# Where a 32x32 transpose takes its stride, and which PSUM bank a fold gives up

## The chip, the core and the metric

One core of a Trainium2 chip runs the whole program. The metric is device time in microseconds, the median of several runs. TensorE (PE) does the matmuls, ScalarE (ACT) and VectorE (DVE) do what lies between them, GpSimd (POOL) does a few subtractions and copies, SyncE (SP) issues most DMAs. PSUM, into which matmuls write, has eight banks of 128 x 512 fp32.

## What is computed

Three stages follow one another; the output of each is the input of the next.

```python
# attention with random features: 2 batches, 8 heads, 576 rows, 64 wide; 128 features
phi(x) = exp(h - max(h)) / sqrt(m),  h = x @ omega.T - sum(x*x)/2
num = phi(q) @ (phi(k).T @ v);  den = phi(q) @ sum(phi(k))
x = num / (den + 1e-6)                       # 1152 x 512
# gated product; w1, w2: 512 x 1024, w3: 1024 x 1024, w_out: 1024 x 512, in 64-bit floats
x = ((x @ w1) * (x @ w2)) @ w3 @ w_out
# four experts, weighted by normalised probabilities p
out = sum over e of p[:, e] * (relu(x @ ew1[e]) @ ew2[e])
```

## The kernel before

Products are computed in three passes over high and low halves of fp32 numbers: `split` (lines 79 to 82) makes a high half with a ScalarE copy and a low half with a VectorE subtraction (in some calls a GpSimd one), both from the same source.

**The attention** works on pairs of heads, eight of them (n = 0 to 7, four per batch). A pair transposes its keys and queries in bank `t`, computes features in the two banks `f`, sums keys with values in `kv`, transposes the exponentials of each of its two heads (`transpose_e`, line 449) in bank `et`, attends (`w` and `po` for the first two pairs, `x` and `kv` from the third), and places the result, transposed in bank `x`, in xt by a split. `attend_tail` does the same for the 64 left-over rows of a batch. A transpose in `et` fills a whole bank with one head, which ScalarE then copies to SBUF.

**The fold** (line 201) multiplies w3 with w_out ahead of time, so that the third stage's input takes one product fewer. There are eight folds, each over 128 rows of w3, in two halves of 12 matmuls into one bank, alternately `po` and `w`; then a split takes the result out of the bank. Each half needs one w3 tile, prepared by `fold_transposed` (line 184): four DMAs of 64-bit numbers, a ScalarE Prelu over the high words (line 100), a VectorE shift of the low words (line 101), a VectorE shift-and-or of the two (line 102), a VectorE transpose of 32x32 blocks (line 194), and a split (lines 81 and 82). Words of a 64-bit number alternate in SBUF, so a reader of the high words steps by 8 bytes. For w3 the columns are also regrouped, every fourth one together (`by_group`), which makes the step of the Prelu and the shift 32 bytes; what they write is contiguous, and so the transpose reads contiguously. The other weights (w1, w2, w_out) go through the same three lines without regrouping, at 8 bytes. Two tiles can stand ready for the fold (`bufs=2`).

**The order** comes from a scheduler that plays the program through with a cost model and takes instructions by priority, each engine's in one fixed order at the end. `BESIDE` (line 41) says which loads (o: w_out, w: w1 and w2), folds (f) and gated products (b) are traced beside which pair: fold 0 beside pair 2, folds 1 to 7 beside pairs 3 to 6, the gated products of batch 0 from pair 7 on, those in banks `w` and `po`. What stands beside a pair may not be issued on VectorE and ScalarE before that pair's query features. After the attention the remaining gated products (in all eight banks), the product with the folded weights, and the experts follow.

Of the kernel before, what the change touches and what calls it, by code (L numbers as in the profile page):

```python
# [8 lines left out]
F32 = mybir.dt.float32  # L9
# [3 lines left out]
ACTF = mybir.ActivationFunctionType  # L13
ALU = mybir.AluOpType
# [31 lines left out]
def attention_moe_kernel(ctx: ExitStack, tc: tile.TileContext, q, k, v, omega, mw1, mw2, mw3, mwo, probs, ew1, ew2, out):  # L46
    nc = tc.nc
# [5 lines left out]
    P = 128  # L53
# [22 lines left out]
    def bank(tag):  # L76
        return ps_p.tile([P, 512], F32, tag=tag, name="ps_" + tag, bufs=BANKS[tag])

    def split(hi, lo, src, eng=None):

        nc.scalar.activation(out=hi, in_=src, func=ACTF.Copy)  # L81
        (eng or nc.vector).tensor_tensor(out=lo, in0=src, in1=hi.bitcast(F32), op=ALU.subtract)  # L82

    def order_like(t, src):
        return t if len(src.shape) == 2 else t.rearrange("p (j g c) -> p j g c", j=src.shape[1], g=src.shape[2])

    def from_f64(srcs, name, order=lambda x: x):


        r = cv.tile([P, 512, 2], U32, tag="f64", name="f64", bufs=3)  # L90
        rows = P // len(srcs)
        for i, src in enumerate(srcs):
            o = r[i * rows:(i + 1) * rows].rearrange("p (k c) w -> p k (c w)", k=src.shape[1])
            nc.sync.dma_start(out=o, in_=src.bitcast(U32))
        low, high = order(r[:, :, 0]), order(r[:, :, 1])
        f = cv.tile([P, 512], F32, tag="f64f", name=name, bufs=2)
        e = cv.tile([P, 512], U32, tag="f64e", name="f64e", bufs=2)
        fb = f.bitcast(U32)

        nc.scalar.activation(out=order_like(f, high), in_=high.bitcast(F32), func=ACTF.Prelu, scale=2.0**-112, alpha=2.0**32)  # L100
        nc.vector.tensor_scalar(out=order_like(e, low), in0=low, scalar1=29, scalar2=None, op0=ALU.logical_shift_right)  # L101
        nc.vector.scalar_tensor_tensor(out=fb, in0=fb, scalar=3, in1=e, op0=ALU.logical_shift_left, op1=ALU.bitwise_or)
        return f

    def load_w64(pool, srcs, name, eng):
        f = from_f64(srcs, name + "f")
        t = pool.tile([P, 2, 512], F32R, tag=pool.name, name=name)
        split(t[:, HI], t[:, LO], f, eng=eng)
        return t
# [5 lines left out]
    def transpose(out, in_, rows=slice(0, P)):  # L115
        return nc.tensor.transpose(out, in_, ident[rows, rows])
# [67 lines left out]
    def fold_transposed(u):  # L184

        m, hf = divmod(u, KF // 4)
        rows = mw3[m * P:(m + 1) * P].rearrange("(j r) f -> r j f", r=SQ)
        first = [hf * 512 + i * P for i in range(4)]  # L190
        by_group = lambda x: x.rearrange("p (j c g) -> p j g c", j=4, g=4)
        r = from_f64([rows[:, :, f:f + P] for f in first], "w3f", by_group)
        t = cv.tile([P, 512], U32, tag="f64e", name="w3t", bufs=2).bitcast(F32)
        nc.vector.transpose(t, r)
        t = t.rearrange("p (j g r) -> p g j r", j=4, g=4)
        wt = cv.tile([P, 2, 512], F32R, tag="w3T", name="w3T", bufs=2)
        hi, lo = (wt[:, x].rearrange("p (g j r) -> p g j r", j=4, g=4) for x in (HI, LO))
        split(hi, lo, t)
        w3T.append(wt)

    def fold(m):

        po = bank(("po", "w")[m % 2])
        n = 0
        for hf in range(KF // 4):
            u = m * (KF // 4) + hf
            while len(w3T) < min(u + 2, KF * (KF // 4)):
                fold_transposed(len(w3T))
            for g in range(4):
                for a, c in PASSES:  # L210
                    nc.tensor.matmul(  # L211
                        out=po, lhsT=w3T[u][:, a, g * P:(g + 1) * P], rhs=wo[hf * 4 + g][:, c],
                        start=(n == 0), stop=(n == 3 * KF - 1),
                    )
                    n += 1
        t = w3_p.tile([P, 2, 512], F32R, tag="w3o", name="w3o", bufs=KF)
        split(t[:, HI], t[:, LO], po)
        w3o.append(t)
# [51 lines left out]
    with ExitStack() as actx:  # L270
# [75 lines left out]
        ps = bank("po")  # L346
# [6 lines left out]
        ps = bank("x")  # L353
# [10 lines left out]
        for b in range(B):  # L364
            t = st.tile([P, H, D1], F32, name=f"vt{b}")
# [18 lines left out]
        class Pair:  # L384
# [62 lines left out]
                nc.scalar.activation(out=self.kva, in_=ps[:, :2 * D1].rearrange("p (j d) -> p j d", j=2), func=ACTF.Copy)  # L447

            def transpose_e(self, j):
                ps = bank("et")  # L450
                self.eT[j] = at.tile([P, MAIN], F32, tag="eT", name="eT", bufs=2)
                for r in range(R):
                    transpose(ps[:, r * P:(r + 1) * P], self.of(self.eq, j, r))
                nc.scalar.activation(out=self.eT[j], in_=ps, func=ACTF.Copy)
# [75 lines left out]
        for n in range(len(pairs) + 1):  # L530
# [32 lines left out]
            with ExitStack() as order:  # L563

                for ins in (*u.mark, loaded) if u else ():
                    order.enter_context(tc.issue_after(ins))
                for s in BESIDE.get(n, "").split():
                    if s[0] == "w":
                        load_w12(int(s[1]))
                    elif s[0] == "o":  # L570
                        load_wo()
                    elif s[0] == "f":
                        fold(int(s[1]))
                    else:
                        gated(at, 2, int(s[1]), int(s[2]), ("w", "po") * 2)
# [319 lines left out]
```

## Time and profile before

| | us |
|---|---|
| median of 3 runs (lowest, highest) | 669.84 (669.25, 671.47) |
| the profiled execution's own time | 670.11 |
| its span, from the first to the last instruction | 668.3 |
| TensorE busy | 655.3 |
| VectorE busy | 463.4 |
| ScalarE busy | 422.0 |
| GpSimd busy | 122.8 |

All instants below count from the first instruction of the profiled execution. A row of the timeline gives start, duration, engine, line, operation, what it writes and reads, its form and how many were merged; in brackets, how long the engine stood idle before it and what released it. PEclk is the clock granted to TensorE as a share of 2.4 GHz; it has two levels, 1.00 and 0.50, and a value between them means that both occurred in the stretch. The merged groups by line give a number of instructions, their busy time and the mean of one, then the idle time before them. Matmuls are pipelined, and the ends of their rows are modelled.

### The profile page before, as it was taken

Reading aid. Unit: us, or ns where it says so; the run is one execution under the profiler, and the core shown is the slowest. Engines: PE = TensorE matmul, PEld = TensorE weight load, DVE = VectorE, ACT = ScalarE, POOL = GpSimd, SP = SyncE. Lnnn points to the kernel's source line nnn. Section 1 sums busy time; section 2 is a strip of 40 time slices with the busy share of each in tenths; the row PEclk is TensorE's granted clock in tenths of the full one; section 3 lists DMA queues with packets and bytes.
Section 4 is the critical chain, followed back from the end, with each engine's and each line's share of the span. In section 5 each row is a group of like instructions: output and inputs, shape, how many; then the busy total and the mean of one; then the engine's idle time right before and its main releaser. Section 6 shows DMA issues by size and latency. Waiting matters only on the chain.

```text
span 668.3 us, 12377 instructions
## 1 busy us (share of the span) xinstructions
PE 655.3 (98%) x4831; PEld 628.2 (94%) x4831; DVE 463.4 (69%) x770; ACT 422.0 (63%) x895; POOL 122.8 (18%) x145
## 2 busy tenths in 40 slices
PE   8999999999999999999999999999999999999997
PEld 6788888899999999999899999999999998999997
DVE  3869867776562134357959868868689588687695
ACT  5899648683552234247768768778587777686740
POOL 2321000131240000000022231331331312314200
PEclk9998999999999999999999999999999999999999
DMA  9868433445110002003154484682883855737725
GB/s 253 268 180 206 122 94 95 127 135 182 59 38 1 1 1 64 1 1 94 64 141 129 65 137 99 113 150 40 157 143 32 152 117 90 138 75 105 126 54 174
DMA packets 58090, 70.59 MB, mean 106 GB/s; under 512 B 8816, under 2 KB 43120, under 8 KB 58032
## 3 DMA queue, kind: packets, MB, share of 16 engines
q1 hardware_dynamic: 44704, 49.05, 25.0%
q0 software_dynamic: 12640, 20.19, 20.6%
q8 instruction: 38, 0.62, 0.4%
q10 hardware_dynamic: 688, 0.56, 0.3%
q14 instruction: 20, 0.16, 0.1%
HBM read 47.24 MB, written 22.54 MB: 104 GB/s over the span
## 4 chain that ended last, share of the span: by engine, by line
PE 82%; DVE 4%; issue 4%; ACT 4%; DMA 3%; POOL 1%; SPq 1%; DVEq 0%; ACTq 0%; POOLq 0%
PE ps_f L807 6%; PE ps_f L725 6%; PE ps_po L211 3%; PE ps_x L725 3%; PE ps_w L725 3%; PE ps_et L725 3%; PE ps_et L807 3%; PE ps_t L807 3%; PE ps_kv L807 3%; PE ps_x L807 3%; PE ps_kv L725 3%; PE ps_t L725 3%; PE ps_po L725 3%; PE ps_w L807 3%; PE ps_w L211 3%
## 5 line engine op out<-in xcount | busy, mean ns | idle before, releaser
L759 POOL DMA_DIRECT2D out_dram<-o x98 | 81.6, 901 | 355.5 <-DVE o L784 173.3
L82 DVE TENSOR_TENSOR hs<-hd,hs 128x1024 fp32r<-128x1024 f32 x48 | 58.3, 1218 | 1.6 <-ACT hs L81 1.6
L81 ACT ACTIVATE hs<-hd 128x1024 fp32r<-128x1024 f32 x48 | 50.6, 1056 | 5.7 <-DVE hd L621 4.6
L709 ACT ACTIVATE hd<-hd 128x288 f32<-128x288 f32 x96 | 40.7, 438 | 9.0 <-DVE hd L707 8.7
L725 PE MATMUL ps_f<-x,w1e 128*128 128x288 f32 x288 | 46.2, 294 | 0.0
L621 DVE TENSOR_TENSOR hd<-hd 128x512 f32<-128x512 f32 x64 | 43.9, 686 | 0.8
L621 DVE TENSOR_TENSOR raw<-raw 128x512 f32<-128x512 f32 x64 | 43.9, 686 | 0.5
L807 PE MATMUL ps_f<-w2e,hs 128*128 128x256 f32 x288 | 43.2, 282 | 0.0
L82 DVE TENSOR_TENSOR w2e<-raw,w2e 128x1024 fp32r<-128x1024 f32 x32 | 38.8, 1218 | 5.4 <-ACT w2e L81 5.3
L725 PEld LDWEIGHTS ps_f<-x,w1e 128*128 128x128 f32 x288 | 40.9, 188 | 0.1
L807 PEld LDWEIGHTS ps_f<-w2e,hs 128*128 128x128 f32 x288 | 38.5, 191 | 0.1
L81 ACT ACTIVATE w2e<-raw 128x1024 fp32r<-128x1024 f32 x32 | 33.1, 1054 | 6.3 <-DVE raw L621 3.2
L168 PE MATMUL ps_po<-xt,w 128*128 128x288 f32 x144 | 35.1, 296 | 0.0
L168 PE MATMUL ps_w<-xt,w 128*128 128x288 f32 x144 | 34.9, 297 | 0.0
L82 POOL TENSOR_TENSOR w<-w12f,w 128x512 fp32r<-128x512 f32 x16 | 22.3, 1404 | 65.4 <-ACT w L81 65.4
L82 DVE TENSOR_TENSOR w1e<-raw,w1e 128x1024 fp32r<-128x1024 f32 x24 | 29.3, 1220 | 5.8 <-ACT w1e L81 5.8
L81 ACT ACTIVATE hid<-a 128x288 fp32r<-128x288 f32 x32 | 13.0, 441 | 29.4 <-DVE a L179 29.2
L101 DVE TENSOR_SCALAR f64e<-f 128x512 uint32<-128x512 uint32 x40 | 24.4, 617 | 9.9 <-DMA f<-in_moe_w_dram 7.2
L81 ACT ACTIVATE w1e<-raw 128x1024 fp32r<-128x1024 f32 x24 | 25.4, 1057 | 6.2 <-issue 2.6
L168 PEld LDWEIGHTS ps_po<-xt,w 128*128 128x128 f32 x144 | 25.6, 189 | 0.1
L168 PEld LDWEIGHTS ps_w<-xt,w 128*128 128x128 f32 x144 | 25.3, 188 | 0.0
L781 ACT ACTIVATE o<-ps_f,pr 128x256 f32<-128x256 f32 (+1 forms) x37 | 17.8, 481 | 11.6 <-PE ps_f L807 7.4
(275 smaller groups left out, 1803.6 us busy)
## 6 DMA issues: line engine op xcount, KB each, us to landing
raw<-in_moe_w_dram SPq DMA_DIRECT2D x32, 512.0 KB, 5.4
out_dram<-o POOLq DMA_DIRECT2D x56, 256.0 KB, 5.1
f<-in_moe_w_dram SPq DMA_DIRECT2D x64, 128.0 KB, 3.3
f<-in_moe_w_dram SPq DMA_DIRECT2D x16, 512.0 KB, 4.6
out_dram<-o POOLq DMA_DIRECT2D x42, 128.0 KB, 4.5
f<-in_moe_w_out_dram SPq DMA_DIRECT2D x8, 512.0 KB, 6.5
kr<-in_k_dram SPq DMA_DIRECT2D x8, 256.0 KB, 5.0
vr<-in_v_dram SPq DMA_DIRECT2D x8, 256.0 KB, 5.1
```

Of the source, the lines that this page charges most:

```text
L81: nc.scalar.activation(out=hi, in_=src, func=ACTF.Copy)
L82: (eng or nc.vector).tensor_tensor(out=lo, in0=src, in1=hi.bitcast(F32), op=ALU.subtract)
L101: nc.vector.tensor_scalar(out=order_like(e, low), in0=low, scalar1=29, scalar2=None, op0=ALU.logical_shift_right)
L168: nc.tensor.matmul(out=bs[c][:, :HS], lhsT=w12[w, g][:, x, kk], rhs=xt[b][kk][:, y, c * HS:(c + 1) * HS], start=(kk == 0 and n == 0), stop ...
L211: nc.tensor.matmul(out=po, lhsT=w3T[u][:, a, g * P:(g + 1) * P], rhs=wo[hf * 4 + g][:, c], start=(n == 0), stop=(n == 3 * KF - 1),)
L621: nc.vector.tensor_tensor(out=o, in0=x, in1=y, op=op)
L709: nc.scalar.activation(out=h, in_=src, func=ACTF.Relu)
L725: nc.tensor.matmul(out=ps, lhsT=w1t[a][:, x, kk, g * P:(g + 1) * P], rhs=x2[b, kk][:, y, s], start=(k in "125" and kk == 0 and n == 0), st ...
L759: dma = nc.gpsimd.dma_start(out=out[toks, d], in_=src[rows], **({} if fresh else dict(accum_op=ALU.add))).ins
L781: nc.scalar.activation(out=o, in_=ps, func=ACTF.Copy, scale=pr[:, t, e:e + 1])
L807: nc.tensor.matmul(out=ps, lhsT=t[a][:, x, g, j * P:(j + 1) * P], rhs=w2t[b][:, y, g], start=(k in "15" and g == 0 and n == 0), stop=(k in ...
```

## The change

`from_f64` loses its `order` argument: Prelu and shift of the w3 tiles read at 8 bytes like those of other weights, and the regrouping passes to the transpose's input, whose innermost step becomes 16 bytes. All folds use bank `po`. The transposes of a pair's second head go to bank `w` from the third pair on; those of the first head, and both heads of the first two pairs, stay in `et`.

```diff
-    def from_f64(srcs, name, order=lambda x: x):
+    def from_f64(srcs, name):
...
-        low, high = order(r[:, :, 0]), order(r[:, :, 1])
+        low, high = r[:, :, 0], r[:, :, 1]
...
-        nc.scalar.activation(out=order_like(f, high), in_=high.bitcast(F32), func=ACTF.Prelu, scale=2.0**-112, alpha=2.0**32)
-        nc.vector.tensor_scalar(out=order_like(e, low), in0=low, scalar1=29, scalar2=None, op0=ALU.logical_shift_right)
+        nc.scalar.activation(out=f, in_=high.bitcast(F32), func=ACTF.Prelu, scale=2.0**-112, alpha=2.0**32)
+        nc.vector.tensor_scalar(out=e, in0=low, scalar1=29, scalar2=None, op0=ALU.logical_shift_right)
...
-        by_group = lambda x: x.rearrange("p (j c g) -> p j g c", j=4, g=4)
-        r = from_f64([rows[:, :, f:f + P] for f in first], "w3f", by_group)
+        r = from_f64([rows[:, :, f:f + P] for f in first], "w3f")
         t = cv.tile([P, 512], U32, tag="f64e", name="w3t", bufs=2).bitcast(F32)
-        nc.vector.transpose(t, r)
+        nc.vector.transpose(t, r.rearrange("p (j c g) -> p j g c", j=4, g=4))
...
-        po = bank(("po", "w")[m % 2])
+        po = bank("po")
...
-                ps = bank("et")
+                ps = bank("w" if j and self.n >= 2 else "et")
```

## Rows read from the trace of the kernel before

**Rows 1.** The page, part 1: busy time, share of the span, instructions of each engine.

```profile
PE 655.3 (98%) x4831; PEld 628.2 (94%) x4831; DVE 463.4 (69%) x770; ACT 422.0 (63%) x895; POOL 122.8 (18%) x145
```

**Rows 2.** Waits of PE, 44 to 165 us: total, times, longest.

```profile
PE ps_x L482 <- DVE xt L82: 0.7, 1, 0.7
PE ps_et L116 <- ACT eq L307: 0.7, 1, 0.7
PE ps_x L461 <- DVE xt L82: 0.4, 1, 0.4
PE ps_f L319 <- ACT eq L332: 0.2, 1, 0.2
```

**Rows 3.** Busy time by stretch: PE, PEld, DVE, ACT, POOL; PEclk, DMA share, GB/s.

```profile
48.00:52.00 4.00, 2.98 (x21) 2.35 (x20) 3.97 (x7) 4.00 (x10) 0.00 (x0) 1.00 1.05 272
52.00:56.00 4.00, 4.00 (x17) 3.40 (x16) 3.75 (x11) 4.00 (x9) 1.74 (x1) 0.57 1.14 218
60.00:92.00 32.00, 32.00 (x176) 26.72 (x175) 29.70 (x61) 20.37 (x35) 0.00 (x0) 1.00 0.56 151
92.00:104.00 12.00, 12.00 (x85) 10.41 (x83) 3.73 (x9) 4.79 (x14) 0.62 (x1) 1.00 0.06 18
160.00:298.00 138.00, 138.00 (x1042) 138.00 (x1042) 58.90 (x124) 49.59 (x115) 11.46 (x8) 1.00 0.08 27
```

**Rows 4.** Groups by line, 47 to 127, 58 to 91 and 136 to 160 us.

```profile
L100 ACT ACTIVATE w3f<-f 128x512 f32<-128x512 f32 x16 | 19.0, 1197 | 0.8 <-DVE d L379 0.6 <-ACT xt L81 0.2
L194 DVE STREAM_TRANSPOSE w3t<-w3f 128x512 f32<-128x512 f32 x16 | 11.3, 706 | 0.2
...
L101 DVE TENSOR_SCALAR f64e<-f 128x512 uint32<-128x512 uint32 x9 | 5.9, 656 | 0.1
...
L100 ACT ACTIVATE w12f<-f 128x512 f32<-128x512 f32 x8 | 5.3, 680 | 0.8 <-POOL w L82 0.7
```

**Rows 5.** Timeline, 44.8 to 51.3 us: a w_out shift, then the stall's rows.

```profile
44.87 0.43 DVE L101 TENSOR_SCALAR f64e<-f 128x512 uint32<-128x512 uint32 x1
...
48.99 1.17 ACT L100 ACTIVATE w3f<-f 128x512 f32<-128x512 f32 x1
...
50.31 0.70 DVE L82 TENSOR_TENSOR xt<-ps_x,xt 128x512 fp32r<-128x512 f32 x1
...
50.47 0.33 PE L116 MATMUL ps_et<-ident,eq 128*128 128x128 f32 x1 [0.66 <-ACT eq L307]
...
51.16 0.41 PE L461 MATMUL ps_x<-kva,eT 128*128 128x65 f32 x2 [0.36 <-DVE xt L82]
```

**Rows 6.** Timeline, 110 to 112 us: a tile's low half, and its first matmul.

```profile
110.06 1.10 DVE L82 TENSOR_TENSOR w3T<-w3t,w3T 128x512 fp32r<-128x512 f32 x1
...
111.21 0.96 PE L211 MATMUL ps_w<-wo,w3T 128*128 128x512 f32 x3
```

**Rows 7.** Busy time of line 211 alone, 59 to 101.4 us: PE, PEld.

```profile
59.00:101.40 42.40, 32.84 (x132) 23.91 (x132) 1.00 0.44 119
```

**Rows 8.** Timeline at two fold boundaries, 67 and 115 us.

```profile
67.50 2.98 PE L211 MATMUL ps_w<-wo,w3T 128*128 128x512 f32 x12
67.56 0.60 ACT L81 ACTIVATE w3o<-ps_po 128x512 fp32r<-128x512 f32 x1 [0.39 <-PE ps_po L211]
68.19 0.69 DVE L82 TENSOR_TENSOR w3o<-ps_po,w3o 128x512 fp32r<-128x512 f32 x1 [1.19 <-ACT w3o L81]
...
114.55 2.18 ACT L332 ACTIVATE ek<-ps_f,mx 128x128 f32<-128x128 f32 x8
115.15 3.01 PE L211 MATMUL ps_po<-wo,w3T 128*128 128x512 f32 x12
...
116.55 0.67 ACT L81 ACTIVATE w3o<-ps_w 128x512 fp32r<-128x512 f32 x1
```

**Rows 9.** Timeline, 143 to 149 us: a pair's transposes, a gated product's last read of w.

```profile
143.33 0.60 PE L116 MATMUL ps_et<-ident,eq 128*128 128x128 f32 x4
...
148.06 0.44 DVE L179 TENSOR_TENSOR a<-ps_w,a 128x288 f32<-128x288 f32 x1
```

More of the change, by code (lines that the diff above doesn't have):

```diff
@@ L82, in split @@
         (eng or nc.vector).tensor_tensor(out=lo, in0=src, in1=hi.bitcast(F32), op=ALU.subtract)
-    def order_like(t, src):
-        return t if len(src.shape) == 2 else t.rearrange("p (j g c) -> p j g c", j=src.shape[1], g=src.shape[2])
-    def from_f64(srcs, name, order=lambda x: x):
+    def from_f64(srcs, name):
         r = cv.tile([P, 512, 2], U32, tag="f64", name="f64", bufs=3)
```

## The prediction

> **What bounds the kernel now.** I read the busy shares first. TensorE is busy 98% of the span, the vector engine 69%, the scalar engine 63% [rows 1]. Both parts of the change act where the w3 tiles are prepared and folded beside the attention, from about 44 to 165 us, and a share over the span says little of that stretch, so the second view was TensorE's waits there: four, 2.0 us together [rows 2]. The third was the busy time by stretch [rows 3]. From 160 to 298 us TensorE is busy 138 of 138 us, so nothing done earlier can shorten that part; it can only let it begin sooner. From 48 to 52 us TensorE is busy 2.98 of 4, and in the next 4 us the granted clock is 0.57: for part of it TensorE ran at 1.2 instead of 2.4 GHz, which costs (1 - 0.57) x 4 = 1.7 us. So all that can be won is about 2.0 + 1.7 = 3.7 us of 668.3, and only if every wait goes. What the change adds has to be measured against a TensorE with no slack.
>
> **Part one: the step moves from the first two readers to the transpose.** Each of the 16 w3 tiles now passes Prelu and shift at a step of 8 bytes instead of 32, and the transpose reads at 16 bytes instead of 4.
> - Prelu: 1.197 us at the 32-byte step; the same shape at 8 bytes takes 0.680 [rows 4]. So 16 x 0.517 = 8.3 us leave the scalar engine.
> - Shift: 0.656 against 0.43 us [rows 4, 5], so 16 x 0.226 = 3.6 us leave the vector engine.
> - Transpose: 0.706 us, contiguous [rows 4]. No row shows it at a step. Below: 0.706, for no layout is easier than a contiguous one, so a gain is excluded. Above: twice that, 1.41. The nearest rows are the two readers at 32 bytes. Prelu lost 0.517 us on 512 elements, about 1 ns an element; the shift lost 0.22. I take Prelu's loss, since the transpose too takes one element after another: 1.2 us, and 16 x 0.5 = 8.0 us come onto the vector engine, net +4.4 us.
>
> On whether 16 bytes is already a long step: the Trainium skill (Advanced Engine Details and Errata, SBUF Cachelines) says that SBUF has 16-byte lines and that an access pays when each element lies in another line, which holds at 16 bytes as at 32. The rows above agree for 32 bytes; for 16 no row shows it. Another page of the Trainium skill (Vector Engine (DVE) Microarchitecture Reference, 5.2 Measured stream behaviour on trn2) gives 1.73 against 1.054 ns per column where one source hops every element; as an estimate the transpose would then take 0.706 + 512 x 0.68 ns = 1.05 us, and the vector engine's net would be +1.9 us instead of +4.4.
>
> What of this is on the path? The w3 tiles mostly wait for TensorE, not it for them. Two places count.
> - 50.47 and 51.16 us. The Prelu at 48.99 stands ahead of the exponentials at which TensorE's 0.7 us wait ends [rows 2, 5]. Half a microsecond less there, however, only brings forward one transpose: the next matmul, at 51.16, is released by the x-split on the vector engine that ends at 51.01 [rows 5]. That queue is shortened by the shift alone. I take -0.2 us, and I leave the slow-clock stretch behind it as it is.
> - 111.21 us. The fold's first matmul follows its tile's low half (110.06 + 1.10 = 111.16) at once [rows 6]. On that tile's chain Prelu gives 0.5, the transpose takes 0.5, and the next tile's shift, queued ahead, gives 0.2: -0.2 us.
>
> Elsewhere the vector engine is the concern. It is busy 29.7 of 32 us between 60 and 92 [rows 3]. Some ten transposes and nine shifts fall in there: +10 x 0.5 - 9 x 0.22 = +3.0, so 32.7 in 32. The 0.7 that doesn't fit moves to 92 to 104, where 8.3 of 12 us are free [rows 3]. I cost it at 0, covered by fold tiles that are ready early; without that cover it is 0.7 us.
>
> **Part two: one bank for all folds.** Fold m+1's first matmul must now wait until fold m's result has left po: the scalar engine's copy, then the subtraction, both reading the bank. At the first boundary fold 1 began at 67.50, while the split of fold 0 ended at 68.19 + 0.69 = 68.88 [rows 8]: 1.38 us. There are seven such boundaries. Behind the waiting matmul stands whatever the scheduler placed after it, so the order itself has to change: attention matmuls must be put there.
> - Six boundaries like the first: 0 if attention fills them, 6 x 1.38 = 8.3 if nothing does. Five lie in 59 to 101.4, where the fold keeps TensorE busy 32.8 of 42.4 us [rows 7]; the other 9.6 are attention, against 5 x 1.38 = 6.9 to be filled, and TensorE never waited there [rows 2], so this work was at hand and stood behind folds. I take 0.5 for all six, near the filled end.
> - Fold 5 to fold 6: fold 6 began at 115.15, but the copy, queued behind exponentials, came only at 116.55 [rows 8]; with 0.67 for it and 0.69 for the subtraction the bank is free at 117.9: 2.8 us late, with attention to fill most of it. 0 to 2.8; I take 0.6.
>
> **Part two: the second head's transposes in w.** From the third pair on they no longer wait for the first head's copy out of et. TensorE's waits name no such case [rows 2], so no gain is booked. But w also carries the gated products. The last pair's transposes, at 143.33 at the latest, come in program order between two gated blocks, so they now wait for the first one's last read of w, at 148.06 + 0.44 [rows 9], and the second block waits for their copy. Other gated blocks in t and f can fill this. Bounds: 0, and 5.2 us (143.33 to 148.5) if nothing fills it. I take 0.2, near the filled end, as TensorE had matmuls at hand there and no wait but the one for the last x-split [rows 2].
>
> Sum: -0.2 - 0.2 + 0 + 0.5 + 0.6 + 0.2 = +0.9 us. The profiled execution took 670.11 us (668.3 between its first and last instruction, 1.8 around it), so 671.0 by its measure; it lies 0.27 above the median of 669.84, so 670.7 us.
>
> **Rivals.**
> - *The starved stretch at 48 to 52 us closes (faster).* For it: it was opened by a scalar engine filled 4.0 of 4 us [rows 3], from which half a microsecond goes, and by attention that a second bank lets run earlier. Against it: the vector engine's x-split holds 51.16. Price: the waits there, 0.7 + 0.4, the slow clock, 1.7, and no boundary loss: 669.8 - 2.8 = 667.0 us.
> - *The folds starve at their boundaries (slower).* One mechanism: po isn't free and no attention matmul is ready. It decides from the point where less than half of the 11.1 us (8.3 + 2.8) is filled. For it: at the last folds attention waits for exponentials itself, 2.18 us of them in a row at 114.55 [rows 8]. Against it: 9.6 us of attention in the main stretch. With half filled: 669.8 + 5.5 - 0.4 = 675 us.
> - *The vector engine becomes the bound (slower).* At 1.41 us a transpose the 32 us from 60 to 92 would have to hold 29.7 + 7.0 - 2.0 = 34.7; if the pairs' maxima and normalisation go late by that, 669.8 + 2.7 + 0.5 = 673 us.
> - *The step costs the transpose nothing.* The Trainium skill (Vector Engine (DVE) Microarchitecture Reference, 3.8 The reshape front-end and per-opcode configuration) describes it as sustaining one element per cycle, which 0.706 us on contiguous data agrees with. Worked from rows: 3.6 us leave the vector engine, the x-split and the tile at 111 come 0.2 to 0.5 earlier, and the boundaries stay: 670 us.
>
> **How the numbers follow.** Forecast 0.42, starved stretch closed 0.20, folds starved 0.20, vector engine bound 0.09, free step 0.09. What this measurement can tell from no change is 0.3%, 2.0 us: 667.8 to 671.9. Faster 0.22 (the first rival and a little of the free step), slower 0.30 (the two slow ones and the forecast's upper edge), same 0.48. The range for 8 in 10 is 667.0 to 675.0. The forecast alone would lie in 669.3 to 672.
>
> **What would show it.** Prelu of w3 near 0.68 and its shift near 0.43; a transpose near 1.2 us; every fold writing po, with other matmuls between the last of one fold and the first of the next; TensorE's waits from 44 to 165 us near 3 us, with new ones that name the fold's split; one slow-clock stretch near 52 us. The prediction is wrong if that stretch is gone, if fold boundaries show idle TensorE of over 1 us each, or if the stretch from 160 us on changes its length.

## The result

The changed kernel is slower: 674.1 us median against 670.44, 18 runs each. The ratio on record, which isn't the quotient of these medians (1.0055), is 1.0052, with a 95% interval of 1.0037 to 1.0067; on 670.4 us that is +3.5 us (2.5 to 4.5). The forecast was +0.9 us. Its sign held and so did its range, but "no change that can be measured" was its likeliest case, and that was wrong.

The changed kernel's profiled execution took 671.25 us, the lowest of its 18 runs (span 669.5, against 668.3 before). So the trace shows a good run of it. Also, it has no slow-clock stretch near 52 us, where the trace of before lost 1.7 us [rows 3]: 1.2 us of span and those 1.7 make, as an estimate, 2.9, close to the 3.5 of the many runs. Over many runs the clock doesn't make the difference: the mean granted clock is 0.9976 over the changed kernel's 18, and 0.9974 to 0.9981 for the kernel before in the three sessions of the experiments.

First the groups by line from 44 to 130 us that answer to [rows 4], with the same columns (lines are three or four lower, since the helper is gone). The last row holds three shifts of other weights too.

```profile
L190 DVE STREAM_TRANSPOSE w3t<-w3f 128x512 f32<-128x512 f32 x16 | 17.7, 1103 | 0.3
...
L97 ACT ACTIVATE w3f<-f 128x512 f32<-128x512 f32 x16 | 10.8, 687 | 3.2 <-DVE w3t L190 2.6 <-DMA f<-in_moe_w_dram 0.5
...
L98 DVE TENSOR_SCALAR f64e<-f 128x512 uint32<-128x512 uint32 x19 | 7.9, 416 | 1.9 <-DMA f<-in_moe_w_dram 1.8
```

Prelu and shift gave up what was forecast, and the transpose rose from 0.706 to 1.10 us. TensorE's waits from 44 to 165 us, the answer to [rows 2]:

```profile
PE ps_po L207 <- DVE w3o L82: 2.8, 2, 1.9
PE ps_x L113 <- DVE xs L376: 1.3, 2, 1.1
PE ps_et L113 <- ACT eq L303: 0.9, 1, 0.9
PE ps_x L457 <- DVE xt L82: 0.5, 1, 0.5
PE ps_t L165 <- POOL w L82: 0.5, 1, 0.5
PE ps_po L207 <- DVE w3T L82: 0.2, 1, 0.2
```

They come to 6.2 us where there were 2.0. Two are new and large: 2.8 us at two fold boundaries (1.9 and 0.8), for the subtraction that frees po, and 1.1 us for the last pair's result. By stretch, as in [rows 3]:

```profile
48.00:52.00 4.00, 2.63 (x17) 1.98 (x16) 3.85 (x9) 3.71 (x12) 1.06 (x1) 1.00 1.10 221
52.00:56.00 4.00, 3.78 (x29) 3.26 (x28) 4.00 (x10) 3.52 (x10) 0.71 (x1) 1.00 1.13 224
60.00:92.00 32.00, 29.25 (x170) 24.82 (x169) 29.64 (x58) 14.93 (x33) 0.00 (x0) 1.00 0.53 139
160.00:298.00 138.00, 138.00 (x1043) 138.00 (x1042) 56.16 (x123) 48.71 (x113) 10.50 (x8) 1.00 0.09 28
```

TensorE lost 2.75 us between 60 and 92, where it had been full, and the stretch from 160 us on is as full as before: what was lost ahead of it stayed lost.

Why the first boundary wait was 1.9 us is seen in the vector engine's timeline of 74 to 79 us:

```profile
74.27 0.19 DVE L593 TENSOR_REDUCE prs<-pr 128x9 f32<-128x36 f32 x1 [1.18 <-issue]
...
75.31 0.42 DVE L98 TENSOR_SCALAR f64e<-f 128x512 uint32<-128x512 uint32 x1
75.64 0.19 DVE L596 TENSOR_TENSOR pr<-pr,prs 128x36 f32<-128x36 f32 x1
75.76 0.69 DVE L99 SCALAR_TENSOR_TENSOR w3f<-w3f,f64e 128x512 uint32<-128x512 uint32 x1
76.49 1.08 DVE L190 STREAM_TRANSPOSE w3t<-w3f 128x512 f32<-128x512 f32 x1
77.49 0.66 DVE L82 TENSOR_TENSOR w3o<-ps_po,w3o 128x512 fp32r<-128x512 f32 x1
```

and, of the other two engines in that stretch:

```profile
74.61 0.60 ACT L81 ACTIVATE w3o<-ps_po 128x512 fp32r<-128x512 f32 x1 [0.82 <-PE ps_po L207]
...
78.20 0.97 PE L207 MATMUL ps_po<-wo,w3T 128*128 128x512 f32 x3 [1.91 <-DVE w3o L82]
```

The copy out of po was done at 75.21. The subtraction could follow then, but it started at 77.49: ahead of it in the queue stood the normalisation of probs, before which the engine had idled 1.18 us (the trace names no releaser; the last piece of probs landed at 74.19, just ahead of 74.27), then a shift, a shift-and-or and a transpose. Attention matmuls filled po's absence up to 76.3, then nothing was ready.

The second boundary wait has another makeup (fold 2's last matmul ends at 83.97):

```profile
83.80 1.00 PE L478 MATMUL ps_x<-kva,eTt 128*128 128x65 f32 x8
...
84.00 0.60 ACT L81 ACTIVATE w3o<-ps_po 128x512 fp32r<-128x512 f32 x1 [1.47 <-PE ps_po L207]
...
84.95 0.64 DVE L82 TENSOR_TENSOR w3o<-ps_po,w3o 128x512 fp32r<-128x512 f32 x1
...
85.65 1.20 PE L207 MATMUL ps_po<-wo,w3T 128*128 128x512 f32 x4 [0.84 <-DVE w3o L82]
```

Here the subtraction followed the copy after 0.35 us. Copy and subtraction took their own time, and attention filled only its first half, up to 84.80.

The last pair, 147 to 158 us (gated product's read of w, transposes into w, copy, attend, normalise, place):

```profile
147.91 0.44 DVE L176 TENSOR_TENSOR a<-ps_w,a 128x288 f32<-128x288 f32 x1
...
149.21 0.60 PE L113 MATMUL ps_w<-ident,eq 128*128 128x128 f32 x4
...
151.15 0.59 ACT L450 ACTIVATE eT<-ps_w 128x512 f32<-128x512 f32 x1
...
153.34 1.00 PE L457 MATMUL ps_kv<-kva,eT 128*128 128x65 f32 x8
...
156.63 0.68 DVE L99 SCALAR_TENSOR_TENSOR w12f<-w12f,f64e 128x512 uint32<-128x512 uint32 x1
157.23 0.15 DVE L374 TENSOR_SCALAR d<-ps_kv 128x4 f32<-128x4 f32 x1
...
157.63 0.42 DVE L376 TENSOR_TENSOR xs<-ps_kv,d 128x256 f32<-128x256 f32 x1
158.11 0.66 PE L113 MATMUL ps_x<-ident,xs 128*128 128x128 f32 x4 [1.07 <-DVE xs L376]
```

The transposes start at 149.21, 5.9 us later than in the kernel before (143.33 [rows 9]), as the wait for w said, and the chain behind them ends in a wait of 1.07 us. Part of that chain is the vector engine's queue again: attending ends at 154.34, but the normalisation of its result starts only at 157.23, behind shifts and ors of w1 and w2 tiles.

### The profile page after: what moved, and what is told of

It is laid out like the page before. It is cut to its first block, busy times and chain, and to the rows that moved or that the text cites. A ratio compares the mean times of both kernels' runs of the same rounds, so it can differ in the third digit from the quotient of the medians.

```text
span 669.5 us, 12370 instructions
## 1 busy us (share of the span) xinstructions
PE 653.0 (98%) x4831; PEld 627.0 (94%) x4831; DVE 463.7 (69%) x770; ACT 414.4 (62%) x895; POOL 121.1 (18%) x145
## 4 chain that ended last, share of the span: by engine, by line
PE 79%; DVE 7%; ACT 5%; DMA 4%; issue 2%; SPq 1%; DVEq 0%; ACTq 0%
PE ps_f L803 6%; PE ps_f L721 6%; PE ps_po L207 4%; PE ps_x L721 3%; PE ps_w L721 3%; PE ps_et L721 3%; PE ps_et L803 3%; PE ps_kv L803 3%; PE ps_t L803 3%; PE ps_x L803 3%; PE ps_kv L721 3%; PE ps_t L721 3%; PE ps_po L721 3%; PE ps_w L803 3%; PE ps_po L803 3%; PE ps_f L165 2%
## 5 line engine op out<-in xcount | busy, mean ns | idle before, releaser
L207 PE MATMUL ps_po<-wo,w3T 128*128 128x512 f32 x192 | 46.8, 396 | 2.9 <-DVE w3o L82 2.8
L207 PEld LDWEIGHTS ps_po<-wo,w3T 128*128 128x128 f32 x192 | 35.3, 188 | 10.4 <-DVE w3o L82 3.0
L82 POOL TENSOR_TENSOR w<-w12f,w 128x512 fp32r<-128x512 f32 x16 | 20.9, 1312 | 64.4 <-ACT w L81 64.4
L98 DVE TENSOR_SCALAR f64e<-f 128x512 uint32<-128x512 uint32 x40 | 19.9, 503 | 9.3 <-DMA f<-in_moe_w_dram 7.4
```

The costliest lines, as they stand in the source:

```text
L98: nc.vector.tensor_scalar(out=e, in0=low, scalar1=29, scalar2=None, op0=ALU.logical_shift_right)
L207: nc.tensor.matmul(out=po, lhsT=w3T[u][:, a, g * P:(g + 1) * P], rhs=wo[hf * 4 + g][:, c], start=(n == 0), stop=(n == 3 * KF - 1),)
```

## The experiments

Theory A: the single fold bank costs the time; A', as a mechanism: through what stands ahead of the releasing instruction in its engine's queue. Theory B: the 1.1 us transposes make the vector engine late. Theory C: gated products hold w when the last pair needs it. All ratios are to the kernel before, run in the same session.

**The step alone.** The diff's first part, banks as before. Each engine's instructions stand in exactly the order of the kernel before, so only durations differ.

> The step alone: transpose at 16 bytes, banks as before. Theory A (the single fold bank costs the time): ratio to before 0.995 to 1.001, since the vector engine's net load (16 x (1.10 - 0.71) - 16 x 0.24 = +2.5 us) is covered and the scalar engine gives up 8 us; TensorE's waits between 44 and 165 us stay near 2 us. Theory B (the longer transpose makes the vector engine late): ratio 1.003 to 1.006, with TensorE waiting 2 us or more for fold tiles or for pairs' normalised results.

Measured: 0.9999 (0.9983 to 1.0015). Its groups by line, 47 to 127 us, show that the durations did change as in the whole change:

```profile
L190 DVE STREAM_TRANSPOSE w3t<-w3f 128x512 f32<-128x512 f32 x16 | 17.6, 1098 | 0.2
...
L97 ACT ACTIVATE w3f<-f 128x512 f32<-128x512 f32 x16 | 10.8, 689 | 4.7 <-DVE w3t L190 1.9 <-DMA pr<-in_moe_domain_probs_dram 1.6 <-DMA f<-in_moe_w_dram 1.3
```

8.1 us off the scalar engine and 2.5 us more on the vector engine moved nothing. Theory B falls as a cause by itself.

**One fold bank alone.**

```diff
-        po = bank(("po", "w")[m % 2])
+        po = bank("po")
```

> All folds in one bank, nothing else changed (32-byte step, transposes of both heads in et). Theory A: ratio 1.003 to 1.007, TensorE waits for a fold's subtraction at two or more of the seven boundaries, 2 to 4 us together. Theory B: at most 1.002, because without the 1.1 us transposes the subtraction runs as soon as the copy is done and each boundary costs under 0.3 us.

Measured: 1.0041 (1.0024 to 1.0058). TensorE's waits for folds, 40 to 170 us:

```profile
PE ps_po L211 <- DVE w3o L82: 2.8, 2, 2.1
PE ps_po L211 <- DVE w3T L82: 1.3, 1, 1.3
```

The same 2.8 us at the same two boundaries (2.1 and 0.7), with transposes of 0.7 us: theory A, and the long transpose isn't needed for it.

**The second head's transposes in w alone**, folds still alternating po and w.

```diff
-                ps = bank("et")
+                ps = bank("w" if j and self.n >= 2 else "et")
```

> Second head's transposes in w from the third pair on, folds still alternating po and w. Theory C (w is held by gated products when the last pair needs it): ratio 1.002 to 1.004, the last pair's second transposes after 147 us instead of 143, and a TensorE wait of about 1 us for that pair's placing near 158 us. If only the fold bank matters: 0.999 to 1.002; but here folds and transposes also share w, which can add waits near 70 to 100 us.

Measured: 1.0071 (1.0047 to 1.0094), more than expected. Here folds and transposes share w as well: fold 5, which began at 98.37 us in the kernel before, began at 107.61. In its trace waits for the pairs' results stand first (from 40 to 170 us), and it has a stretch of half clock from about 100.0 to 110.3 us. That execution was the slowest of the run's six, but the clock was low in the others too: their mean granted clock is 0.9942, against 0.9977 for the kernel before, which as an estimate makes 0.0035 x 670 = 2.3 of the 4.8 us lost. So the edit isn't harmless. Nor is it shown that giving up w in the fold helps it: with both edits (the next run) the ratio isn't apart from this one.

```profile
PE ps_et L116 <- DVE xs L380: 1.3, 1, 1.3
PE ps_et L116 <- ACT eq L307: 1.0, 1, 1.0
PE ps_x L116 <- DVE xs L380: 0.7, 1, 0.7
PE ps_x L461 <- ACT eT L454: 0.7, 1, 0.7
```

**Both bank edits, no step.** Instructions in exactly the whole change's order.

> Both bank edits, the step left where it was. Theory A with C: ratio 1.003 to 1.007, as the whole change. Theory B: 0.999 to 1.002. The sum of the log ratios of this and of the step alone should come near the whole change's 1.0052 if the parts don't interact.

Measured: 1.0066 (1.0039 to 1.0092). The banks make the loss; with 0.9999 for the step the parts add up to the whole's 1.0052 within their intervals. The two bank edits don't add up: 1.0041 and 1.0071 alone would make 1.011 together.

**The last pair back in et** (the whole change else).

```diff
-                ps = bank("w" if j and self.n >= 2 else "et")
+                ps = bank("w" if j and 2 <= self.n < 7 else "et")
```

> The whole change, but the last pair's second head is transposed in et again, so that it needs no bank that gated products hold. Theory C (w held by gated products costs 1 to 2 us at the end of the attention): ratio to before 1.002 to 1.004, and the 1.1 us wait for that pair's placing near 158 us is gone. If the fold bank is all of it: 1.004 to 1.007, as the whole change. The waits for the folds' subtractions, 2.8 us, stay in both.

Measured: 1.0042 (1.0021 to 1.0063): lower than the whole, but not apart from it. The wait near 158 us is gone, and another of 1.8 us came near 163 (for the split of the last x), so the trace by itself doesn't settle theory C. The waits for the folds' subtractions didn't stay at 2.8 us: they are 3.5 here, 2.7 of them at the boundary where the normalisation of probs stands in the queue, before which the vector engine idled 2.00 us.

**The result leaves po by one copy.**

```diff
-        split(t[:, HI], t[:, LO], po)
+        c = cv.tile([P, 512], F32, tag="w3c", name="w3c", bufs=1)
+        nc.scalar.activation(out=c, in_=po, func=ACTF.Copy)
+        split(t[:, HI], t[:, LO], c)
```

> The whole change, but a fold's result leaves po by one scalar-engine copy to SBUF, and high and low half are made from that copy; 8 x 0.6 us more on the scalar engine. Theory A' (a boundary costs what it does because the subtraction, which frees the bank, stands in the vector engine's queue): the 2.8 us waits for the subtraction vanish, TensorE waits at most 0.5 us for the copy, ratio 0.999 to 1.003. If the boundary is slow because a single bank leaves TensorE without ready work whatever frees it: waits of 2 us or more remain under another name, ratio 1.004 to 1.007.

Measured: 1.0039 (1.0021 to 1.0058), between the two expectations, and the waits didn't vanish: 2.2 us, now for the copy, which is the sign that was named for the other case. The profiled execution was the slowest of the run's twelve (677.14 us). The larger wait, in the timeline of 84 to 87 us:

```profile
85.43 0.67 ACT L97 ACTIVATE w3f<-f 128x512 f32<-128x512 f32 x1 [3.60 <-DVE w3t L190]
86.01 0.57 ACT L214 ACTIVATE w3c<-ps_po 128x512 f32<-128x512 f32 x1
...
86.64 1.09 PE L207 MATMUL ps_po<-wo,w3T 128*128 128x512 f32 x2 [1.47 <-ACT w3c L214]
```

The copy stood behind a Prelu for which the scalar engine had idled 3.60 us, until a transpose gave back the Prelu's buffer. So here it is the place in a queue, now the scalar engine's, that sets the release. That is A', though the expectation that named this remedy enough was wrong. The smaller wait, 0.71 us at 115.21, isn't of that kind: its copy began at 114.55, 0.05 us after the fold's last matmul, and TensorE had nothing else ready while it ran.

**Both remedies.**

> Both remedies: the result leaves po by one copy, and the last pair's second head stays in et. If theories A' and C name all of the loss: ratio 0.996 to 1.001, with TensorE's waits from 40 to 170 us at 2 us or less. If attention pulled ahead into the fold gaps is missing later: 1.002 to 1.005.

Measured: 1.0018 (1.0002 to 1.0035). Better than the whole change, above the expected 1.001 by its middle; the fold still waits 2.1 us for the copy.

**Probs late.** The ten DMAs of probs are issued after the last w1/w2 tile, and the vector engine normalises them then. No order but SP's and the vector engine's differs. In the cut below `loads64[-1]` is the last DMA that `from_f64` issued; the lines that keep that list are left out.

```diff
-        order.enter_context(tc.issue_after(pairs[-1].loaded))
+        order.enter_context(tc.issue_after(loads64[-1]))
```

On the whole change:

> The whole change; the ten pieces of probs are loaded, and so normalised on the vector engine, after the last w1/w2 tile instead of near 75 us; TensorE's and the scalar engine's orders stay what they are. In the whole change the vector engine stood 1.2 us waiting for these pieces ahead of the subtraction that frees po, and took 0.9 us for them. Theory A' (the bank is freed late because of what stands in the vector engine's queue): the fold waits fall from 2.8 to about 1 us, ratio to before 1.001 to 1.004. If the queue would be as late without them: 1.004 to 1.007.

Measured: 1.0025 (1.0004 to 1.0046), as A' expected, though its interval overlaps that of the whole change. The waits for the subtraction, which were 2.8 us, are

```profile
PE ps_po L209 <- DVE w3o L82: 1.2, 2, 0.9
```

Only the first boundary gained: its subtraction started 0.72 us after the copy instead of 2.28, and its wait fell from 1.91 to 0.34 us. The second, where the queue wasn't the cause, kept 0.86. So, in these two executions, A' accounts for about 1.6 of the 2.8 us; the rest is the time of copy and subtraction for which no attention was left.

On the step alone:

> The step alone, with the same move of probs. Here no fold waits for the vector engine, so the queue has nothing to give: by theory A' 0.998 to 1.001, as the step alone. Below 0.997 would say that the vector engine's queue held TensorE up in the kernel before too, and would make this a kernel faster than both.

Measured: 0.9994 (0.9977 to 1.0011). Where no fold waits for the queue, emptying it wins nothing that can be told, so it isn't shown to beat the kernel before.

On both remedies:

> Result leaves po by one copy, last pair's second head in et, and probs late: what was left of the loss with both remedies was 1.0018. By theory A' the rest lay in the vector engine's queue as well: 0.998 to 1.001. If attention taken early into the fold gaps is missing later: 1.001 to 1.004.

Measured: 1.0004 (0.9986 to 1.0022), and of the 2.1 us for the copy

```profile
PE ps_po L209 <- ACT w3c L216: 0.7, 1, 0.7
```

is left, the copy's own time at one boundary. With the place in the queue, the release and the last pair's bank all mended, the new banks cost nothing that can be measured, and win nothing either.

**No regrouping at all.** Contiguous 32-column blocks for the transpose, w_out's rows loaded to match, banks as before. TensorE, ScalarE, VectorE and GpSimd have the order of the kernel before. The cut is against the changed kernel; the two bank edits, taken back, are left out.

```diff
-        rows = mwo[hf * 512:(hf + 1) * 512].rearrange("(p g) d -> g p d", g=4)[g]
-        wo.append(load_w64(w1_p, [rows.unsqueeze(1)], "wo", nc.gpsimd))
+        rows = mwo[hf * 512:(hf + 1) * 512].rearrange("(i g c) d -> g i c d", i=4, g=4)[g]
+        wo.append(load_w64(w1_p, [rows[i].unsqueeze(1) for i in range(4)], "wo", nc.gpsimd))
...
-        nc.vector.transpose(t, r.rearrange("p (j c g) -> p j g c", j=4, g=4))
+        nc.vector.transpose(t, r)
```

> Banks as before; no regrouping of w3's columns anywhere: w_out's rows are loaded in the order that contiguous blocks need (four DMAs of 128 KB for each of the eight w_out tiles instead of one of 512 KB). Prelu 0.69, shift 0.42 and transpose 0.71 us at once, so 8 us less on the scalar and 3.6 us less on the vector engine. If TensorE alone bounds this stretch, as the step alone at 0.9999 says: 0.997 to 1.001. If the vector engine's load held something up: below 0.997. The 24 more DMA issues on SP may cost up to 1 us early.

Measured: 1.0038 (1.0019 to 1.0057), outside both expectations. With the orders the same and the three readers faster, the loads of w_out are what is left to cost time, more than the estimate of 1 us; by which path isn't shown further than this: the last w_out tile landed at 40.34 us (37.85 before), its Prelu began at 50.38 us (47.48 before), TensorE was busy 10.20 of 12 us from 20 to 32 (10.66 before), with a stretch of half clock, and fold 0 began at 60.48 instead of 58.84. The half clock isn't of this execution alone: the mean granted clock is 0.9952 over the twelve runs, against 0.9974 for the kernel before, as an estimate 0.0022 x 670 = 1.5 of the 2.5 us lost. That the scalar and the vector engine became freer by some 11 us shows nowhere.

## Why the prediction was right and wrong

- **What bounds the kernel.** Right: TensorE had no slack, the stretch from 160 us on stayed at 138 of 138 us, and relieving the scalar engine by 8 us was worth nothing that can be measured (0.9999). The two gains of 0.2 us that I booked are too small for that interval; near 50 us the step alone shows the exchange that I described without its gain: the wait for the exponentials fell from 0.7 to 0.2 us, and the next one, for the x-split, rose from 0.4 to 0.9.
- **The transpose.** I took 1.2 us; it is 1.10. The estimate of 1.05 us from the Trainium skill's page Vector Engine (DVE) Microarchitecture Reference (5.2) was nearer. Sixteen bytes between elements is already a long step: the Trainium skill's rule of 16-byte lines (Advanced Engine Details and Errata, SBUF Cachelines) agrees with the 1.10 us here, and the rival of a free step is out. The 0.706 us that I called in agreement with one element per cycle is 1.38 ns an element over the whole instruction; no run here tells how much of that is one cycle, so that agreement isn't shown. Net on the vector engine: 16 x (0.397 - 0.24) = +2.5 us, not +4.4, and covered, as I had it: in the step alone the vector engine was busy 30.74 of 32 us between 60 and 92, and TensorE 32.00.
- **Fold boundaries.** This is the step that failed: 0.5 + 0.6 = 1.1 us taken, 2.8 us of waits in the profiled execution. I priced the wait as copy plus subtraction back to back, 1.38 us, from [rows 8], and then assumed that attention would fill it. At five of seven boundaries it did; at 78.20 and 85.65 us attention had been used up by the gap itself. At 78.20 the gap was also longer than I had it, for the subtraction came 2.28 us after the copy: I had counted the vector engine's load (29.7 of 32 us) but not what it means for one instruction that now had somebody waiting behind it; [rows 8] showed a vector engine that had idled 1.19 us ahead of the subtraction. At 85.65 copy and subtraction came nearly as priced, and half of their time stayed unfilled. Nor were six boundaries like the first: in the kernel before, fold 6's result left its bank at 127.35 us, 4.46 us after fold 7 had begun at 122.89. That didn't cost anything, as in the changed order fold 7 began at 127.90, without a wait. The rival "the folds starve" had the mechanism and the sign; its price of 5.5 us, half of all gaps unfilled, was too high.
- **The w bank.** The place and the time were right (transposes to 148.5; they began at 149.21), and the 0.2 us were mis-sized: a wait of 1.07 us at the chain's end, since what is late is not the transposes alone but the pair's last placing, whose normalisation stood in the vector engine's queue. How much of the loss it makes by itself isn't settled: without it 1.0042 against 1.0052.
- **The slow-clock stretch.** I left it in place, and in the profiled execution it was gone, although TensorE was busy only 2.63 of 4 us ahead of it, less than before. That was one of my signs of being wrong, as was a boundary with over 1 us of idle TensorE (one of the two, with 1.9). The stretch isn't a term of either kernel, though: over the changed kernel's 18 runs the granted clock goes from 0.992 to 1.000 (and see below).
- **What stays open.** Of the loss, 1.0018 is left with both remedies and 1.0004 with probs late too; the steps between single remedies are smaller than their intervals. That the banks cost the time is shown, and so are its two ways at the fold boundaries; the share of each part, above all of the w bank, is not.

## What to carry to other kernels

A buffer that loses its double can be as late as the place of the releasing instruction in its engine's queue makes it, and not only as late as that instruction takes: look up what stands ahead of it, DMA waits of unrelated work included. And where TensorE is full, don't count the same work at hand for every gap: here seven gaps in a row found enough for five.

## What the runs showed beside

The slow-clock stretch near 52 us comes and goes with the same instructions in the same order on TensorE and the scalar engine. Busy time by stretch (columns as in [rows 3]) of the step alone, which has the whole order of the kernel before:

```profile
48.00:52.00 4.00, 2.90 (x22) 2.45 (x21) 3.97 (x7) 4.00 (x13) 0.73 (x1) 1.00 1.09 236
52.00:56.00 4.00, 4.00 (x31) 3.64 (x31) 4.00 (x12) 3.06 (x8) 0.55 (x1) 1.00 1.15 217
```

and of the step with probs late:

```profile
48.00:52.00 4.00, 2.41 (x18) 1.94 (x16) 3.74 (x7) 3.88 (x12) 0.49 (x1) 0.98 1.05 249
52.00:56.00 4.00, 4.00 (x17) 3.46 (x17) 3.48 (x11) 2.67 (x6) 0.80 (x1) 0.59 1.06 224
```

The clock fell in the second and in the kernel before, and stayed at 2.4 GHz in the first and in the whole change. TensorE's busy time in the 4 us ahead doesn't order them: 2.41 and 2.98 us where it fell, 2.90 and 2.63 where it did not. The spans of these two executions are 665.5 us (the step alone, the fastest of its 12 runs) and 668.5 us; of the 3.0 us between them the half clock makes, by the rows above, (0.02 + 0.41) x 4 = 1.7. Single executions of one kernel lie further apart still: the step alone's 12 runs go from 667.29 to 672.88 us, more than the effect studied here. Only the many runs told the kernels apart.
